# Landmark sums of five batches taken from a second load of q and k

## The chip, the cores and the metric

The kernel runs on one NeuronCore of a Trainium2 chip. Its engines are TensorE (PE in the profile; its weight loads, PEld, overlap its products), VectorE (DVE), ScalarE (ACT), GpSimd (POOL) and SyncE (SP), and 16 DMA engines that move data between HBM and SBUF. The metric is the device time of one execution in microseconds (us); lower is better. The kernel before took 270.38 us, the median of three runs of 268.30, 270.38 and 270.43 us.

## The reference

Nyström attention over 8 batches of 8 heads, 576 tokens and 64 features, then a two-layer feed-forward with a squared ReLU over 4,608 tokens, all in float32 at the interface. Cut to what matters:

```python
m = 32                                                   # landmarks: 576 / 32 = 18 tokens each
q_lm = q.reshape(B, H, m, S // m, D).mean(axis=3)
k_lm = k.reshape(B, H, m, S // m, D).mean(axis=3)
A  = softmax(scale * q @ k_lm.T)                         # 576 x 32
Bm = softmax(scale * q_lm @ k_lm.T)                      # 32 x 32
C  = softmax(scale * q_lm @ k.T)                         # 32 x 576
Z = Bm.T / (norm1(Bm) * norminf(Bm) + 1e-6)              # norms over the last two axes
for _ in range(6): Z = 2 * Z - Z @ Bm @ Z
attn = A @ Z @ C @ v                                     # heads side by side: 512 features
h = attn @ w_in; r = maximum(h, 0); out = (r * r) @ w_out   # 512 -> 2048 -> 512
```

The change is about the first step, the mean over each 18 neighbouring tokens: it makes the 32 landmarks of every head.

## The kernel before

The work goes batch by batch. The 8 heads of a batch sit as four heads by two halves `r`: 128 partitions are four heads (`c`) of 32 segments each, and one partition holds the 18 tokens of its segment side by side, 18 x 64 elements. `load_qk` brings q or k of one half into the tile `X` in that form (`ldq5.1` is q of batch 5, half 1), cast to bf16 on the way. `X` has three buffers, so batches 3 and 6 use that of batch 0. `load_v` does the same for v (`ldv5.10`), `load_win` and `load_wout` load the weights. All loads are issued by POOL, in the order of its program, and run through one software DMA queue; the finished rows of the output go out through SP's queue.

For a batch `b` the steps are:

- `lm{b}`: landmark sums on PE. The 18 tokens of a partition are added by products with an identity, in the 64x64 tiling of the array: 36 products of 256 columns (line 480, `X` against `ident`), which leave two half sums in different partitions. `lmc` (two copies, line 379 on ACT or 383 on DVE, into `LS`) and `lme` (line 498 on DVE) add them and scale; `lmt` transposes them into `LT`. Batches 0 and 1 do some of this in the full array (line 473).
- `T{b}`: four 32x32-block transposes of `X` into `TT` on DVE (line 441).
- `B{b}` and the small steps behind it: softmax and norm of the 32 x 32 matrices; then six rounds of the iteration, `N{b}.i` on PE (line 666) and `U{b}.i` on DVE (line 680). From batch 2 on each round needs `bd{b}.i`, a block-diagonal copy that POOL or DVE makes (line 603).
- `SS{b}`: the scores for A and C on PE (lines 697, 702), their softmaxes on DVE and ACT; `CV{b}` (line 788) is C v, `ZC{b}` Z times that, and `W{b}` in four chunks (line 859) its product with `w_in`, copied to `WP`: the first layer then multiplies A by `WP` and the attention output is never formed.
- `F{b}`: the first layer on PE (line 1023), `R` the ReLU (line 1037 on ACT, 1039 on DVE), `Q` its square (1044, 1046); `O{t}`: the second layer for output tile `t` of 128 tokens, four groups of four products (line 1063), `Oe` the copy out of PSUM, `St` the store.

What runs in which order is written out by hand: the string `ORDER` names every step, PE's products of one batch between the chains of the next. `Plan.schedule` walks through it with a table of costs, gives each step a start on its engine, and the instructions are emitted by these starts; so each engine executes one fixed sequence, and an engine whose next instruction has to wait holds up all behind it. A load can only be issued by POOL when its buffer is free and when the load eight places before it has landed (`SW_LANES`). Until the first `O` the plan puts dummy products (`fill`, line 1137) into PE's gaps.

`add_landmarks` and `landmarks_added`, another way to make the sums, stand in the file before, but no batch uses them (`ADDED` is empty).

Of the kernel before, what the change touches and what calls it, by code (L numbers as in the profile page):

```python
# [7 lines left out]
P = 128  # L8
# [8 lines left out]
H = 8  # L17
S = 576
D = 64
# [34 lines left out]
class Plan:  # L54
# [42 lines left out]
    def schedule(self, order):  # L97
# [5 lines left out]
        for word in order:  # L103
# [33 lines left out]
            if o.queue == "hw":  # L137
                o.end = free[e] + (self.LANDS_LOADED if t < LOADED else self.LANDS)
            elif o.nbytes:
                sw = max(sw, free[e] + 0.5)  # L140
                sw += o.nbytes / (RATE["sw"] if sw < 23.0 else RATE["later"])
                o.end = sw + LAND
                landed.append(o.end)
# [37 lines left out]
RATE = {"sw": 0.375e6, "later": 0.405e6, "hw": 0.2e6}  # L181
# [55 lines left out]
def kernel(  # L237
# [13 lines left out]
    def mk(name, shape, dt):  # L251
        return sb.tile(shape, dt, name=name, tag=name)
# [17 lines left out]
    LD = [mk(f"LD{i}", [P, 2, 2, 6, D], F32) for i in range(2)]  # L270
# [30 lines left out]
    ident = mk("ident", [P, P], BF16)  # L301
    blk2 = mk("blk2", [P, 2, M], BF16)
# [25 lines left out]
    def c_sel(e):  # L328
# [4 lines left out]
                                channel_multiplier=-1)  # L333
    op("c5", {"POOL": 0.5}, c_sel, R=["onesf"], W=["msel"])
# [58 lines left out]
    def add_landmarks(b):  # L393
        for s in range(SEG // 6):
            for t in range(2):
                src = (q, k)[t][b].rearrange("(r c) (m s) d -> (c m) r (s d)", r=2, s=SEG)
                kd = ("LD", b % 2, t)

                def add(e, s=s, t=t, src=src):
                    nc.gpsimd.dma_start(LD[b % 2][:, t].rearrange("p r j d -> p r (j d)"),  # L400
                                        src[:, :, 384 * s:384 * s + 384],
                                        **({"accum_op": ALU.add} if s else {}))
                op(f"la{b}.{s}{t}", {"POOL": 0.74}, add, R=[kd] if s else [], W=[kd],
                   nbytes=900000 if s else 425000, queue="sw")
# [26 lines left out]
    def attention(b):  # L431
# [17 lines left out]
        def landmarks_added():  # L449
            ls = LS[i2].rearrange("p r n -> p (r n)")[:, 0:256].rearrange("p (t r d) -> p t r d", t=2, d=D)  # L450
            ld, kd, kS = LD[i2], [("LD", i2, t) for t in range(2)], ("LS", i2, 0)
            for t in range(2):
                op(f"lmc{b}.{t}", {"DVE": v_(384), "POOL": g_(384)}, lambda e, t=t: eng(e).tensor_tensor(
                    ld[:, t, :, 0:3], ld[:, t, :, 0:3], ld[:, t, :, 3:6], ALU.add),
                   R=[kd[t]], W=[kd[t]], port=("POOL", "DVE"))
                op(f"lmd{b}.{t}", {"DVE": v_(128), "POOL": g_(128)}, lambda e, t=t: eng(e).tensor_tensor(
                    ls[:, t], ld[:, t, :, 0], ld[:, t, :, 1], ALU.add),
                   R=[kd[t]], W=[(kS, t)], port=("POOL", "DVE"))
                op(f"lmf{b}.{t}", {"DVE": v_(128), "POOL": g_(128)}, lambda e, t=t: eng(e).tensor_tensor(
                    ls[:, t], ls[:, t], ld[:, t, :, 2], ALU.add),  # L460
                   R=[kd[t], (kS, t)], W=[(kS, t)], port=("POOL", "DVE"))
            op(f"lme{b}.0", {"ACT": 0.36, "DVE": 0.25}, lambda e: copy(e, lm[:], ls, scale=LMS),
               R=[(kS, 0), (kS, 1)], W=[("LM", i2, r) for r in range(2)])
# [636 lines left out]
    def loads(what, b):  # L1100
# [9 lines left out]
        elif what == "la":  # L1110
            add_landmarks(b)
# [9 lines left out]
    for b in range(B):  # L1121
        if b in ADDED:
            loads("la", b)
# [29 lines left out]
ADDED = ()  # L1153
# [16 lines left out]
c0 ldq0.0 c1 c17 Bce0@4 c12 ldk0.0 ldq0.1 ldk0.1 c5 c6 ldk1.0 ldq1.1 ldk1.1 c2 ldq1.0 c15 c9 c13  # L1170
T0.00 c3 lm0.0@5 T0.10 lme0.0/D lmt0.0 SC0.0@6 T0.01 T0.11 lm0.1@0 lmc0.10 Cmx0.0 Cex0.0 c11 win01
ldv0.11 ldv0.10 lmc0.11/D lme0.1 lmt0.1 bk0/P ldv0.00 win30 win10 win11 win00 ldv1.00 win31 ldq2.1
win21 ldq2.0 T1.10 B0@2 Bmx0 Bsb0 T1.01 Bex0 SC0.1@0 Cmx0.1 Cex0.1 Bsu0 Brc0 SA0.0@7 Amx0.0b Bml0
Bmb0 Asb0.0b Aex0.0b Btr0 SA0.1@2 Amx0.1b Bcs0 CT0.0 Asu0.0b Bnm0 Crc0 Amx0.1a Brn0 c10 Cmk0
BBT0@0 Arc0.0b Yi0 Zi0 T1.00 lm1.0@6 N0.0@0 U0.0 N0.1@0 lme1.0 lmt1.0 Amx0.0a bk1/P win20 ldk2.1
ldk2.0 ldv1.10 ldv1.11 U0.1 B1@4 Aml0.0b Bmx1 N0.2@6 U0.2 Asb0.0a Bsb1 Asb0.1a CT0.1 Aex0.0a CR0@1
CRe0/A Bex1 Aex0.1a c14/A N0.3@4 U0.3 Asu0.0a Bsu1 N0.4@5 U0.4 N0.5@0 Brc1 Arc0.0a Bml1 Asb0.1b
Aex0.1b Bmb1 U0.5 Blo1 Btr1 CV0@4,6 CVe0.1/A Aml0.0a Zd0@1 Zm0 Asu0.1a Bcs1@0 BBT1@3 Ap0.0@7 Bnm1
Arc0.1a Bad1 Aml0.1a Asu0.1b Brn1 Arc0.1b Zi1 Yi1 T1.11 CVe0.0/A ZC0@5 Ab0.0/A SA1.1@0 ZCe0 W0.0@6
We0.01 We0.00 N1.0@3 U1.0 Aml0.1b Amx1.1 W0.1@4 We0.1 N1.1@3 U1.1 Ap0.1@6 Ab0.1/A SA1.0@2 Asb1.1  # L1180
Aex1.1 N1.2@3 U1.2 Amx1.0 SC1.0@6,4 Cmx1.1 wout0 wout1 F0.2@0 R0.2 N1.3@3 U1.3 Cex1.1 F0.0@0 R0.0
# [120 lines left out]
```

## Time and profile before

| | us |
|---|---|
| median of three runs | 270.38 (268.30 to 270.43) |
| the profiled execution: its time | 271.93 |
| its span, first to last instruction | 270.2 |
| PE busy in it | 250.8 |
| DVE, ACT, POOL busy | 211.9, 186.5, 61.3 |
| granted PE clock, mean | 0.994 |

The span is 1.7 us shorter than the execution's time, and that execution took 1.55 us more than the median. "Busy" counts the time in which at least one instruction runs. The profile's views used below are: the page with its groups by line; the waits, by what ended each idle stretch of an engine; the chain of work that ended last, in order of time; the timeline of one engine; tables of windows (busy time of each engine in a stretch, then the granted PE clock, the DMA share and the GB/s written); and the DMA's packets and bytes in a window.

### The profile page before, as it was taken

How to read it: one execution, taken by the hardware profiler on the slowest of the kernel's cores; microseconds unless marked ns; L12 is line 12 of the kernel's file. 1: busy time of each engine (PE TensorE's matmuls, PEld its weight loads, DVE VectorE, ACT ScalarE, POOL GpSimd, SP SyncE). 2: the span in 40 equal slices, each digit the busy share in tenths (PEclk: the TensorE clock that was granted, in tenths of full speed). 3: DMA queues.
4: the chain of work that ended last, by engine and by line, in shares of the span. 5: the costliest groups of instructions: out<-in, count | busy, mean ns of one | idle time of the engine just before them, and what ended most of it. 6: DMA issues, size and time to landing. Idle time of an engine off the chain costs nothing.

```text
span 270.2 us, 7623 instructions
## 1 busy us (share of the span) xinstructions
PE 250.8 (93%) x3111; PEld 143.2 (53%) x3149; DVE 211.9 (78%) x562; ACT 186.5 (69%) x334; POOL 61.3 (23%) x101
## 2 busy tenths in 40 slices
PE   6888899999999499999999999999999999999993
PEld 2455566475454256546455656556454565556542
DVE  3799997867999659968998999897999988662320
ACT  1344797799594579778597688889773887795121
POOL 8366495623250000130201101002201000000000
PEclk9999999999999989999999999999999999999999
DMA  6999999979599470359410433003244300006145
GB/s 108 203 187 207 208 207 208 206 135 181 114 168 217 107 126 2 52 86 226 100 41 2 76 90 71 13 0 83 61 100 67 96 2 2 0 0 154 43 98 136
DMA packets 17282, 28.27 MB, mean 105 GB/s; under 512 B 2272, under 2 KB 6624, under 8 KB 17248
## 3 DMA queue, kind: packets, MB, share of 16 engines
q0 software_dynamic: 11328, 18.35, 41.1%
q1 hardware_dynamic: 5840, 9.38, 13.1%
q8 instruction: 24, 0.39, 0.6%
q10 hardware_dynamic: 80, 0.07, 0.1%
q14 instruction: 10, 0.08, 0.1%
HBM read 36.70 MB, written 9.44 MB: 171 GB/s over the span
## 4 chain that ended last, share of the span: by engine, by line
PE 62%; DVE 14%; DMA 10%; ACT 5%; issue 4%; POOL 3%; POOLq 0%; ACTq 0%; DVEq 0%
PE ps L1063 34%; PE ps L1023 18%; DMA X<-in_q_dram 10%; ACT RS L1037 3%; PE ps L859 3%; POOL X L390 2%; PE ps L788 1%; DVE ST L680 1%; PE ps L480 1%; DVE SA L976 1%; DVE sm L740 1%; DVE RS L1039 1%; PE ps L702 1%; DVE smA L979 1%; PE ps L666 1%
## 5 line engine op out<-in xcount | busy, mean ns | idle before, releaser
L1063 PE MATMUL ps<-w_out,G 128*128 128x512 bf16 (+1 forms) x558 | 134.1, 374 | 3.6 <-issue 2.1
L1063 PEld LDWEIGHTS <-G 128*128 128x128 bf16 x592 | 54.8, 98 | 56.4 <-issue 7.9
L1023 PE MATMUL ps<-AT,WP 128*128 128x288 bf16 (+2 forms) x512 | 75.5, 288 | 0.7 <-ACT RS L1037 0.5
L1037 ACT ACTIVATE RS<-ps 128x576 bf16<-128x576 f32 (+2 forms) x95 | 59.7, 652 | 15.1 <-PE ps L1023 13.9
L1023 PEld LDWEIGHTS <-WP 128*128 128x128 bf16 x512 | 48.4, 98 | 22.5 <-issue 2.8
L1044 ACT ACTIVATE G<-RS 128x576 bf16<-128x576 bf16 (+2 forms) x74 | 49.5, 683 | 7.8 <-DVE RS L1039 7.0
L377 ACT CAST WP<-ps 128x1024 bf16<-128x1024 f32 (+1 forms) x30 | 28.0, 972 | 5.1 <-PE ps L859 3.5
L1039 DVE TENSOR_SCALAR RS<-ps 128x576 bf16<-128x576 f32 (+1 forms) x33 | 24.3, 744 | 7.1 <-PE ps L1023 5.6
L1046 DVE TENSOR_TENSOR G<-RS 128x576 bf16<-128x576 bf16 (+2 forms) x45 | 19.9, 452 | 12.3 <-ACT RS L1037 11.9
L441 DVE STREAM_TRANSPOSE TT<-X 128x576 uint32<-128x576 uint32 x32 | 24.2, 762 | 3.6 <-DMA X<-in_q_dram 2.6
L603 POOL TENSOR_TENSOR BD<-ST,blkb 128x256 bf16<-128x256 bf16 x13 | 9.1, 704 | 78.3 <-DVE ST L680 72.7
L377 ACT COPY OS<-ps 128x512 f32<-128x512 f32 (+2 forms) x26 | 14.6, 561 | 15.6 <-PE ps L1063 14.9
L743 ACT ACTIVATE C<-ps,sm 128x576 bf16<-128x576 f32 x16 | 14.4, 905 | 8.3 <-DVE sm L740 8.0
L680 DVE SCALAR_TENSOR_TENSOR ST<-ST,ps 128x128 bf16<-128x128 bf16 (+1 forms) x48 | 12.7, 265 | 8.0 <-PE ps L666 6.6
L412 POOL DMA_DIRECT2D V<-in_v_dram x24 | 12.9, 539 | 15.5 <-PE ps L788 12.0
L381 DVE COPY OS<-ps 128x512 f32<-128x512 f32 (+1 forms) x12 | 7.8, 647 | 10.3 <-PE ps L1063 6.6
L390 POOL DMA_DIRECT2D X<-in_k_dram x16 | 9.0, 561 | 17.3 <-DVE sm L754 16.1
L740 DVE TENSOR_REDUCE sm<-ps 128x1 f32<-128x576 f32 x16 | 11.8, 742 | 0.8 <-PE ps L702 0.8
L1137 PE MATMUL ps<-onesb 128*128 128x512 bf16 (+1 forms) x35 | 10.3, 406 | 2.0 <-DVE onesb L319 1.5
L379 ACT ACTIVATE LS<-ps 64x256 f32<-64x256 f32 (+1 forms) x8 | 2.9, 366 | 12.1 <-PE ps L480 12.0
L480 PE MATMUL ps<-X,ident 64*64 64x256 bf16 (+1 forms) x252 | 7.8, 264 | 3.6 <-DMA X<-in_q_dram 3.1
L390 POOL DMA_DIRECT2D X<-in_q_dram x16 | 9.2, 573 | 8.2 <-DVE sm L597 5.5
(131 smaller groups left out, 298.9 us busy)
## 6 DMA issues: line engine op xcount, KB each, us to landing
out_dram<-OS SPq DMA_DIRECT2D x70, 128.0 KB, 2.6
X<-in_q_dram POOLq DMA_DIRECT2D x16, 288.0 KB, 7.2
X<-in_k_dram POOLq DMA_DIRECT2D x16, 288.0 KB, 7.6
V<-in_v_dram POOLq DMA_DIRECT2D x8, 288.0 KB, 6.6
w_in<-in_moe_w_in_dram POOLq DMA_DIRECT2D x8, 256.0 KB, 10.0
w_out<-in_moe_w_out_dram POOLq DMA_DIRECT2D x4, 512.0 KB, 10.8
V<-in_v_dram POOLq DMA_DIRECT2D x8, 216.0 KB, 5.3
V<-in_v_dram POOLq DMA_DIRECT2D x8, 72.0 KB, 2.6
```

Source lines behind the costliest of these rows:

```text
L377: nc.scalar.copy(o, i)
L390: lambda e: nc.gpsimd.dma_start(x[:, t, r].rearrange("p s d -> p (s d)"), src),
L441: op(f"T{b}.{t}{r}", {"DVE": v_(576)}, lambda e, r=r: nc.vector.transpose(tt[:, t, r].rearrange("p s m e -> p (s m e)").bitcast(U32), x[:, ...
L680: nc.vector.scalar_tensor_tensor(out=o, in0=i0, scalar=2.0, in1=bank(pN)[:, 0:2 * w].rearrange("p (r w) -> p r w", r=2), op0=ALU.mult, op1 ...
L740: op(f"Cmx{b}.{r}", {"DVE": v_(576)}, lambda e, r=r: nc.vector.tensor_reduce(s_[:, 12 + r:13 + r], cbanks(r), axis=AX.XY, op=ALU.max, nega ...
L743: op(f"Cex{b}.{r}", {"ACT": a_(576) + 0.27}, lambda e, r=r: nc.scalar.activation(Cs[r][:].rearrange("p x u -> p u x"), cbanks(r), AF.Exp, ...
L1023: nc.tensor.matmul(ps[:, ph.at + i, 0:w], lhsT=wp[:, r, 128 * ff:128 * ff + 128], rhs=at[:, r, t0:t0 + w], start=(r == 0), stop=(r == 1))
L1037: nc.scalar.activation(rs, pair(ph, w), AF.Relu)
L1039: nc.vector.tensor_scalar(out=rs, in0=pair(ph, w), scalar1=0.0, scalar2=None, op0=ALU.max)
L1044: nc.scalar.activation(g, rs, AF.Square)
L1046: eng(e).tensor_tensor(g, rs, rs, ALU.mult)
L1063: nc.tensor.matmul(bank(po)[:, 0:c1 - c0], lhsT=G[:, f, lo:lo + P], rhs=w_out[:, f, c0:c1], start=(f == 0), stop=(f == NF - 1))
```

## The change

For batches 3 to 7 (`ROWS`) the landmark sums no longer come from `X`. A new load, `lx{b}.0` for q and `lx{b}.1` for k, brings the whole of q and of k a second time, in another form, into a new tile `XS` of 96 partitions: partition `p` holds tokens 6p to 6p + 5 of each of the 8 heads. Three neighbouring partitions are then one segment. `lm{b}.0` becomes 24 products in the 128x32 tiling (four column tiles, one for each head `c`): the stationary operand is `seg`, a 96 x 32 matrix of ones and zeros, the moving one token of the six for that head of q and k and both halves, 256 columns, and six products add up in one PSUM bank. One copy with a scale, `lme`, takes the result to `LM`; the two `lmc` copies and the addition are gone for these batches. `XS` has one buffer: `lx4` can only be issued when `lm3` is done. `X` is still loaded for all batches, for the transposes. `LD`, a tile of the unused way, is removed and has the same size in total.

Beside it the plan's table gets a third, lower rate for loads after 48 us, and `ORDER` is searched anew: all 1,420 words of it stand elsewhere, in the early part too. In it the half r = 1 of batch 0 comes first, and of the block-diagonal copies 25 are on POOL where 15 were (on DVE 17 where 27 were). ACT gets 97 of the ReLU steps where it had 95 and 78 of the squares where it had 74.

```diff
-RATE = {"sw": 0.375e6, "later": 0.405e6, "hw": 0.2e6}
+RATE = {"sw": 0.375e6, "hw": 0.2e6, "first": 0.375e6, "then": 0.405e6, "late": 0.29e6}
...
-    LD = [mk(f"LD{i}", [P, 2, 2, 6, D], F32) for i in range(2)]
+    XS = mk("XS", [96, 2, H, 6, D], BF16)
...
+    def load_xs(b):
+        for t in range(2):
+            src = (q, k)[t][b].rearrange("h (p j) d -> p h (j d)", j=6)
+            op(f"lx{b}.{t}", {"POOL": 0.57}, lambda e, t=t, src=src: nc.gpsimd.dma_start(
+                XS[:, t].rearrange("p h j d -> p h (j d)"), src),
+               W=[("XS", t)], nbytes=1179648, queue="sw")
...
+        def landmarks_rows():
+            pl_ = Bank(1, "att")
+            view = lambda: bank(pl_)[:, 0:256].rearrange("p (t r d) -> p t r d", t=2, d=D)
+
+            def lmx(e):
+                xs = XS[:].rearrange("p t (r c) j d -> p t r c j d", r=2)
+                for j in range(6):
+                    for c in range(4):
+                        nc.tensor.matmul(view()[quad(c)], lhsT=seg[:], rhs=xs[:, :, :, c, j, :],
+                                         start=(j == 0), stop=(j == 5))
+            op(f"lm{b}.0", {"PE": pe(256, 6) + 0.11}, lmx, R=["seg", ("XS", 0), ("XS", 1)], W=[pl_],
+               alloc=[pl_], mode="128x32", ni=48)
+            op(f"lme{b}.0", {"ACT": 0.1 + ap_(256), "DVE": v_(256)},
+               lambda e: copy(e, lm[:], view(), scale=LMS), R=[pl_], W=[("LM", i2, r) for r in range(2)])
...
-            if b in ADDED:
-                landmarks_added()
+            if b in ROWS:
+                landmarks_rows()
...
     for b in range(B):
-        if b in ADDED:
-            loads("la", b)
+        if b in ROWS:
+            loads("xs", b)
...
-ADDED = ()
+ROWS = (3, 4, 5, 6, 7)
...
-c0 ldq0.0 c1 c17 Bce0@4 c12 ldk0.0 ldq0.1 ldk0.1 c5 c6 ldk1.0 ldq1.1 ldk1.1 c2 ldq1.0 c15 c9 c13
+c0 ldq0.1 c1 c2 ldk0.1 c3 lm0.1@2 lmc0.10 c12 T0.01 c17 Bce0@5 ldq0.0 ldk0.0 ldq1.0 ldk1.0 c5
```

PE's sequence where the sums of batch 4 begin. Before, they follow the second chunk of `W2` and read `X_63`, the buffer of batch 4:

```order
2399 L859 Ldweights ZC_0_92
2400 L859 Matmult ps<-w_in,ZC_0_92 32x512
2401 L859 Ldweights ZC_1_93
2402 L859 Matmult ps<-w_in,ZC_1_93 32x512
2403 L480 Ldweights ident
2404 L480 Matmult ps<-X_63,ident 64x256
2405 L480 Ldweights ident
2406 L480 Matmult ps<-X_63,ident 64x256
```

With the change they follow the first round of batch 3's iteration (`N3.0`), ahead of `W2`, and read `XS`:

```order
2337 L666 Ldweights BD_101
2338 L666 Matmult ps<-ST_0_99,BD_101 128x64
2339 L666 Ldweights BD_101
2340 L666 Matmult ps<-ST_0_99,BD_101 128x64
2341 L458 Ldweights seg
2342 L458 Matmult ps<-XS,seg 32x256
2343 L458 Ldweights seg
2344 L458 Matmult ps<-XS,seg 32x256
```

So the product that the next batch hangs on now stands ahead of `W2` instead of behind half of it, and needs another load.

POOL's sequence of loads before that point. Before, behind the block-diagonal copy for batch 3 (row 60); `X_63` is batch 4's buffer, `X_62` batch 6's, `X_64` batch 5's:

```order
60 L603 TensorTensor BD_103<-Bt_114,blkb 128x256
61 L412 DMACopy V_67<-in_v_dram 96x1152
62 L412 DMACopy V_66<-in_v_dram 128x1152
63 L390 DMACopy X_64<-in_k_dram 128x1152
64 L412 DMACopy V_65<-in_v_dram 96x1152
65 L390 DMACopy X_62<-in_q_dram 128x1152
66 L390 DMACopy X_62<-in_k_dram 128x1152
67 L390 DMACopy X_63<-in_q_dram 128x1152
68 L390 DMACopy X_64<-in_k_dram 128x1152
69 L390 DMACopy X_63<-in_q_dram 128x1152
70 L390 DMACopy X_63<-in_k_dram 128x1152
```

With the change (row 64 is the same copy; rows 61 and 63 are `lx4.0` and `lx4.1`, rows 69 and 71 `lx5.0` and `lx5.1`):

```order
60 L413 DMACopy V_67<-in_v_dram 96x1152
61 L403 DMACopy XS<-in_q_dram 96x8x384
62 L413 DMACopy V_65<-in_v_dram 128x1152
63 L403 DMACopy XS<-in_k_dram 96x8x384
64 L603 TensorTensor BD_102<-Bt_113,blkb 128x256
65 L397 DMACopy X_63<-in_k_dram 128x1152
66 L397 DMACopy X_63<-in_q_dram 128x1152
67 L603 TensorTensor BD_101<-ST_0_99,blkb 128x256
68 L397 DMACopy X_64<-in_q_dram 128x1152
69 L403 DMACopy XS<-in_q_dram 96x8x384
70 L603 TensorTensor BD_102<-ST_1_100,blkb 128x256
71 L403 DMACopy XS<-in_k_dram 96x8x384
72 L413 DMACopy V_66<-in_v_dram 96x1152
```

Where nine loads stood in one piece behind the copy, the two for batch 4's sums now stand ahead of it, two of batch 4's four `X` loads behind it, and the rest are spread between copies.

More of the change, by code (lines that the diff above doesn't have):

```diff
@@ L140, in schedule @@
                 sw = max(sw, free[e] + 0.5)
-                sw += o.nbytes / (RATE["sw"] if sw < 23.0 else RATE["later"])
+                sw += o.nbytes / RATE["first" if sw < 23.0 else "then" if sw < 48.0 else "late"]
                 o.end = sw + LAND
@@ L1175 @@
[L1175 to L1180, printed above, removed]
```

223 lines of the change are left out of this document (105 added, 118 removed).

## The prediction

> **What bounds the kernel now.** I read the page first, then PE's waits after its first second-layer product, then the chain around the one long wait.
>
> ```profile
> PE 250.8 (93%) x3111; PEld 143.2 (53%) x3149; DVE 211.9 (78%) x562; ACT 186.5 (69%) x334; POOL 61.3 (23%) x101
> PEclk9999999999999989999999999999999999999999
> ...
> PE ps L480 <- DMA X<-in_q_dram: 3.1, 1, 3.1
> PE ps L1063 <- issue: 2.1, 12, 0.3
> ...
> 44.42 0.59 PE ps L1063 x2
> ...
> 77.31 14.98 DMA X<-in_q_dram
> 92.54 1.18 PE ps L480 x36
> ...
> 113.94 1.11 PE ps L480 x36
> 115.04 0.56 PE ps L859 x16
> ...
> 135.37 0.49 PE ps L1023 x4
> 135.86 1.73 PE ps L1063 x8
> ```
>
> PE is busy 93% of the span. From 44.42 us, the first `O`, it waits 3.1 us once for a load and 2.1 us in twelve scraps of at most 0.3 us: from there on the kernel lasts as long as PE's work plus that one hole. The hole is `lm4.0` at 92.54 us: it needs all of batch 4's `X`, and the last part, q of half 0, took 15 us from its issue. The table of 1-us windows shows the hole and what follows; columns are the length, PE, PEld, DVE, ACT and POOL busy, the granted PE clock, the DMA share and GB/s.
>
> ```profile
> 89.00:90.00 1.00, 0.39 (x16) 0.09 (x7) 1.00 (x3) 0.98 (x2) 0.00 (x0) 1.00 0.97 250
> 90.00:91.00 1.00, 0.00 (x0) 0.00 (x0) 0.55 (x2) 1.00 (x2) 0.00 (x0) 1.00 0.42 103
> 91.00:92.00 1.00, 0.00 (x0) 0.00 (x0) 0.00 (x0) 0.16 (x1) 0.00 (x0) 1.00 0.12 25
> 92.00:93.00 1.00, 0.46 (x17) 0.49 (x21) 0.68 (x1) 0.00 (x0) 0.00 (x0) 1.00 0.00 0
> 93.00:94.00 1.00, 0.71 (x28) 0.57 (x21) 0.96 (x4) 0.24 (x1) 0.00 (x0) 0.84 0.07 16
> 94.00:95.00 1.00, 0.96 (x3) 0.40 (x3) 0.14 (x1) 0.14 (x1) 0.98 (x2) 0.50 0.09 23
> 95.00:96.00 1.00, 1.00 (x5) 0.50 (x4) 0.00 (x0) 0.43 (x1) 0.09 (x1) 0.50 1.00 150
> 96.00:97.00 1.00, 1.00 (x6) 0.60 (x4) 0.00 (x0) 0.57 (x2) 0.00 (x0) 0.50 0.97 99
> 97.00:98.00 1.00, 1.00 (x10) 0.75 (x9) 0.53 (x2) 0.75 (x3) 0.00 (x0) 0.95 1.02 171
> ```
>
> PE stands still from 89.39 to 92.54 (3.15 us). Then its clock falls to half: 0.84, 0.50, 0.50, 0.50 and 0.95 in five windows are 1.71 us of missing clock, of which I count 1.6, since PE was idle for part of the first. The hole costs **4.75 us** in all.
>
> [...]
>
> **Part 1: the products.** Five times 36 products (1.11 to 1.18 us in the chain, mean 1.15) give way to five times 24. Four column tiles should run side by side, as eight small tiles do in line 859: 16 products of 512 columns in 0.56 us, where one after the other four products of 288 columns take 0.49 us, so 16 of 512 would take 3.5. Six rounds of 256 columns are then 6 x 0.109 (0.49 / 4 x 256 / 288) = 0.65 us; the old form had 9 x 0.109 = 0.98 and took 0.17 more, so I take 0.82. Bounds: 0.65, and 24 x 0.109 = 2.6 if they don't overlap at all. Gain 5 x 0.33 = **1.65 us**, all on PE's path; at 2.6 it would be a loss of 7.3.
>
> **Part 2: the hole.** `lm4.0` no longer waits for `X`. It needs `lx4.0` and `lx4.1`, which stand ahead of the long row of loads. Whether the hole closes or only moves is a question of the queue:
>
> ```profile
> DMA packets 815, 1.66 MB, mean 184 GB/s; under 512 B 89, under 2 KB 89, under 8 KB 815
> q0 software_dynamic: 763, 1.56, 101.9%
> ...
> DMA packets 1648, 1.66 MB, mean 208 GB/s; under 512 B 51, under 2 KB 1644, under 8 KB 1646
> ...
> q0 software_dynamic: 11328, 18.35, 41.1%
> q1 hardware_dynamic: 5840, 9.38, 13.1%
> ...
> V<-in_v_dram POOLq DMA_DIRECT2D x8, 72.0 KB, 2.6
> ```
>
> The first two rows are 76 to 85 us, where only `X` and `v` were loaded: 1.56 MB in 9 us, 173 GB/s, so an `X` part of 0.295 MB takes 1.7 us. The third is 39 to 47 us, packets of 1 KB (`w_out`): 208 GB/s. An `lx` is 768 packets of 768 bytes, 0.59 MB: 2.9 us at 205 GB/s, **3.4 us** at 173, which I take. The far bound is the mean over all software packets: 41.1% of 16 x 270.2 us by 11,328 is 157 ns each, 7.5 us for 768 of them on 16 engines. Output rows take 13.1% of 270.2 us, 35 us spread over the 225 behind 44 us: 16%, so I divide by 0.84. A small load lands 2.6 us after issue, 0.4 of it bytes: 2.2 us fixed.
>
> When each sum is due comes from adding the PE rows above, and those of the other groups, along the new order from its first `O` (which stands behind 26.1 us of PE work, before behind 25.9, so I leave it at 44.4): `lm3.0` at 62.6, `lm4.0` 87.9, `lm5.0` 103.1, `lm6.0` 149.0, `lm7.0` 169.6. (The same addition over the old order gives 90.5 for `lm4.0`, where the trace, without the hole, has 89.4.)
>
> - `lx3.1`: about 34.5 `X` parts' worth is queued up to it, against 30.2 up to `wout3`, whose bytes end near 47; two `lx` and a quarter part behind it land by 57. Margin 6 us.
> - `lx4.1`: from 62.5 us there are 4.75 parts of `X` and v and two `lx`: (4.75 x 1.7 + 2 x 3.4) / 0.84 + 2.2 puts it at 82. Margin 5 us.
> - `lx5.1` is the tight one. `lx5.0` can't be issued before `lm4.0` has read `XS`. Between the two stand 15.2 us of PE work (6 groups of `O`, 11 `F`, 4 chunks of `W`, 5 rounds `N`, `B4`, `CV3`, `lm4`); the queue needs 0.6 + 2.2 + (1.7 + 2 x 3.4) / 0.84 = 12.9. Margin 2.3 us: it holds up to 4.4 us for an `lx`.
> - `lx6.0` and `lx7.1` hold up to 4.9 and 5.2 us by the same sum.
>
> [...]
>
> So both items of the hole go: **4.75 us**. What comes next late? PE's other waits came to 2.5 us over 225, and I take 0.7 us for waits of the new order that the old one lacked (bounds 0, and 4.75 for another hole of that size).
>
> **Part 3: what lies beside.** Costed at nothing:
>
> ```profile
> L379 ACT ACTIVATE LS<-ps 64x256 f32<-64x256 f32 (+1 forms) x8 | 2.9, 366 | 12.1 <-PE ps L480 12.0
> L390 POOL DMA_DIRECT2D X<-in_q_dram x16 | 9.2, 573 | 8.2 <-DVE sm L597 5.5
> L427 POOL DMA_DIRECT2D w_out<-in_moe_w_out_dram x4 | 3.1, 771 | 1.9 <-DMA X<-in_q_dram 1.2 <-DMA w_in<-in_moe_w_in_dram 0.6
> L603 POOL TENSOR_TENSOR BD<-ST,blkb 128x256 bf16<-128x256 bf16 x13 | 9.1, 704 | 78.3 <-DVE ST L680 72.7 <-DVE Btf L549 5.6
> L603 DVE TENSOR_TENSOR BD<-ST,blkb 128x256 bf16<-128x256 bf16 x23 | 6.5, 281 | 0.4
> ...
> 130.00:140.00 10.00, 9.89 (x114) 4.94 (x104) 9.54 (x25) 7.05 (x14) 1.05 (x3) 1.00 0.42 95
> 190.00:200.00 10.00, 9.79 (x116) 4.99 (x116) 9.90 (x24) 7.64 (x14) 1.84 (x3) 1.00 0.48 102
> ```
>
> Ten `lmc` copies of 0.37 us go and the chain from `lm` to `B` gets shorter; ACT and DVE have this room already. Ten block-diagonal copies move from DVE (0.28 us) to POOL (0.70): DVE loses 2.8 us of work, ten rounds get 0.42 us longer each, hidden by the `O` and `F` groups between `N`s; without that cover 4.2 us. DVE is the engine near its limit (9.54 and 9.90 of 10 us), and it only gets lighter. Ten more loads cost POOL some 0.9 us each (0.57 at 128 rows, 0.77 at 512, on that slope 0.91 at 768): 9 us on an engine that is busy 23%. But POOL is in order: a load that waits for `lm`, or for the load eight places back, now stands ahead of more block-diagonal copies. DMA share falls to 0.42 and 0.48 in the two windows, so 34 us more of loads fit.
>
> In the first 44 us the same loads run ahead of `wout3`, the halves of batch 0 change places, and one block copy of 1.2 us goes from POOL to DVE. I take 0, bounds 1.4 either way (one `X` part in the queue).
>
> **Sum**, against the profiled execution: 271.93 - 1.65 - 4.75 + 0.7 = 266.2 us. That execution took 1.55 us more than the median, so the forecast is **264.7 us**. Its own range, from the bounds of products, head and waits without a new hole, is 262 to 267.
>
> **Rivals.**
>
> - *The hole moves.* A sum or a transpose waits 3 us or more somewhere else, most likely at `lm5.0` (margin 2.3 us) or where DVE takes `T4.01`, whose load comes some eight parts later. It gives back 2 to 4.75 us and some of the next engine's time: 267 to 270. For it: the old order, too, was laid out for its loads to be in time and missed by 3 us. Against: the new order has a lower rate for late loads, and the margins above.
> - *Slow short packets (slower).* At L us for an `lx`, `lm5`, `lm6` and `lm7` each wait 2.38 us for every us above 4.4, 4.9 and 5.2. At 5.6 us the gain of 5.7 is gone; at 6.0 it is 273; at the far bound of 7.5 these three alone cost 7.4 + 6.2 + 5.5 = 19 us, 284. Only the mean per packet speaks for it; the 1-KB window speaks against, 78 ns a packet (8 us x 16 / 1,646), which is 3.7 us.
> - *The change doesn't do what it says*: the four column tiles run one after the other. Then 7.3 us lost where I have 1.65 gained: 273.7. Line 859's rows speak against it, though they show 64-row tiles.
> - *More gain*: no new waits and an earlier head, 261 to 262.
>
> **How the numbers follow.** The forecast 0.62, the moved hole 0.18, slow packets 0.10, serial tiles 0.05, more gain 0.05. A measurement here tells some 1% from no change: under 267.7 is faster, over 273.1 slower. Faster: forecast, more gain and a small part of the moved hole, 0.70. Within 1%: the rest of it and the mild end of slow packets, 0.17. Slower: the rest, 0.13. Forecast and moved hole hold 0.80: 261.5 to 270.
>
> **What would show it.** Right: no PE wait over 1 us after the first `O`; clock 1.00 around 90 us; the new products in 0.7 to 0.9 us; `XS` landing 6 to 8 us after issue when queued. Wrong: a wait of PE for `XS` or of DVE for `X`, with a half-clock stretch behind it; products near 2.6 us; the first `O` later than 46 us; POOL's copies late behind a waiting load.

## The result and the profile after

The changed kernel takes 267.97 us, the median of 20 runs (265.46 to 269.84); the kernel before, run beside it, took 270.40 (20 runs, 268.30 to 274.24). The ratio is 0.9913, with a 95% interval of 0.9888 to 0.9938: 2.4 us faster. (The ratios here and below leave out single runs that lie more than 1.5% above the fastest of the same kernel.) The prediction was 264.7 us, 5.7 us faster than before, in a range of 261.5 to 270.0. The direction and that range hold; the narrower range of 262 to 267, for a change without a new hole, doesn't. Less than half of the gain came: 267.97 lies within 1% of the time before, to which the prediction gave 0.17.

The profiled execution of the change took 268.07 us, its span is 266.3. First the page's rows for the engines and for the granted PE clock, then PE's waits from 40 us to the end (us in total, times, longest):

```profile
PE 254.8 (96%) x3090; PEld 140.4 (53%) x3090; DVE 210.7 (79%) x539; ACT 185.9 (70%) x339; POOL 75.1 (28%) x121
...
PEclk9799999999999999999999999999999999999999
```

```profile
PE ps L1023 <- DVE AT L996: 0.3, 1, 0.3
PE ps L1023 <- ACT CV L384: 0.2, 1, 0.2
```

Behind the first `O` PE waits 0.5 us in all: the hole at `lm4.0` is gone and no other took its place. The dip of the clock that stood at 92 us is gone too. There is a new one, in the second slice of the span, ahead of 14 us. The chain that ended last (start, length, what) shows what came before it, and the new products:

```profile
2.36 6.80 DMA X<-in_k_dram
9.30 0.70 PE ps L480 x36
...
63.48 0.77 PE ps L458 x24
...
89.77 0.77 PE ps L458 x24
```

The sums take 0.77 us where the old form took 1.11 to 1.18. The chain's first piece is the second load of the program, k of batch 0: issued at 2.36, landed at 9.16. The timeline of the kernel before has the start of the transpose that reads that load, and PE's first `O`; the timeline of the change has the same two rows (start, length, engine, line, operation, and in brackets the idle time ahead and what ended it):

```profile
7.10 0.78 DVE L441 STREAM_TRANSPOSE TT<-X 128x576 uint32<-128x576 uint32 x1 [0.47 <-DMA X<-in_k_dram]
...
43.99 1.02 PE L1063 MATMUL ps<-w_out,G 128*128 128x512 bf16 x3 [0.22 <-ACT RS L1037]
```

```profile
9.19 0.78 DVE L442 STREAM_TRANSPOSE TT<-X 128x576 uint32<-128x576 uint32 x1 [2.75 <-DMA X<-in_k_dram]
9.30 0.70 PE L480 MATMUL ps<-X,ident 64*64 64x128 bf16 x36 [2.19 <-DMA X<-in_k_dram]
...
45.94 1.03 PE L1063 MATMUL ps<-w_out,G 128*128 128x512 bf16 x4
```

The load comes 2.1 us later, PE stands still for 2.2 us for it, and the first `O` comes 1.95 us later. (The 44.42 of the prediction was a piece of the chain that starts inside the first group; by the timeline that group starts at 43.99, and from here on all kernels are read by the timeline.) The windows of the change, in the prediction's columns, show the clock at half speed for 3.4 us, from 1 us behind the end of the stall:

```profile
10.00:11.00 1.00, 1.00 (x5) 0.46 (x6) 0.68 (x4) 0.27 (x1) 0.23 (x2) 0.63 1.07 196
11.00:12.00 1.00, 1.00 (x7) 0.16 (x8) 0.90 (x2) 0.00 (x0) 0.80 (x3) 0.50 1.14 214
12.00:13.00 1.00, 1.00 (x17) 0.40 (x16) 0.00 (x0) 0.00 (x0) 0.54 (x1) 0.50 1.10 207
13.00:14.00 1.00, 1.00 (x13) 0.67 (x10) 0.82 (x2) 0.03 (x1) 0.34 (x1) 0.67 1.08 205
```

So the time splits at the first `O`. Before it lies the **head**: 43.99 us before, 45.94 now. Behind it lies the **stretch** to the end of the span: 270.2 - 43.99 = 226.2 before, 266.3 - 45.94 = 220.4 now. The stretch gained 5.8 us and the head gave 1.95 back.

### The profile page after: what moved, and what is told of

It is laid out like the page before. It is cut to its first block, busy times and chain, and to the rows that moved or that the text cites. A ratio compares the mean times of both kernels' runs of the same rounds, so it can differ in the third digit from the quotient of the medians.

```text
span 266.3 us, 7555 instructions
## 1 busy us (share of the span) xinstructions
PE 254.8 (96%) x3090; PEld 140.4 (53%) x3090; DVE 210.7 (79%) x539; ACT 185.9 (70%) x339; POOL 75.1 (28%) x121
## 4 chain that ended last, share of the span: by engine, by line
PE 73%; DVE 13%; ACT 6%; issue 3%; DMA 3%; POOL 0%; DVEq 0%; POOLq 0%; ACTq 0%
PE ps L1063 40%; PE ps L1023 20%; ACT RS L1037 3%; DMA X<-in_k_dram 3%; PE ps L859 2%; PE ps L702 2%; DVE TT L442 2%; PE ps L788 2%; ACT G L1044 2%; PE ps L1137 1%; DVE sm L740 1%; DVE WP L388 1%; DVE ST L680 1%; PE ps L666 1%; DVE An L938 1%
## 5 line engine op out<-in xcount | busy, mean ns | idle before, releaser
L1063 PE MATMUL ps<-w_out,G 128*128 128x512 bf16 (+1 forms) x592 | 138.5, 374 | 0.1
L1023 PEld LDWEIGHTS <-WP 128*128 128x128 bf16 x512 | 47.9, 98 | 23.8 <-issue 4.3
L1044 ACT ACTIVATE G<-RS 128x576 bf16<-128x576 bf16 (+2 forms) x78 | 52.3, 687 | 0.7
L603 POOL TENSOR_TENSOR BD<-ST,blkb 128x256 bf16<-128x256 bf16 x21 | 14.9, 710 | 85.6 <-DVE ST L680 44.1
L1039 DVE TENSOR_SCALAR RS<-ps 128x576 bf16<-128x576 f32 (+2 forms) x31 | 23.1, 754 | 5.4 <-PE ps L1023 5.1
L384 ACT CAST WP<-ps 128x1024 bf16<-128x1024 f32 (+1 forms) x25 | 22.8, 949 | 3.3 <-PE ps L859 3.2
L1137 PE MATMUL ps<-onesb 128*128 128x512 bf16 (+1 forms) x40 | 14.1, 470 | 1.8 <-DVE onesb L320 1.5
L976 DVE STREAM_TRANSPOSE SA<-ps 128x320 f32<-128x320 f32 (+1 forms) x24 | 10.1, 459 | 3.5 <-PE ps L697 2.4
L603 POOL TENSOR_TENSOR BD<-Bt,blkb 128x256 bf16<-128x256 bf16 x4 | 3.0, 744 | 30.9 <-DVE sm L597 15.0
L1046 POOL TENSOR_TENSOR G<-RS 128x512 bf16<-128x512 bf16 (+1 forms) x8 | 8.8, 1101 | 9.3 <-DVE RS L1039 5.9
L388 DVE CAST WP<-ps 128x1024 bf16<-128x1024 f32 x9 | 10.8, 1205 | 0.8 <-PE ps L859 0.8
```

The source lines that it names most:

```text
L384: nc.scalar.copy(o, i)
L388: eng(e).tensor_copy(o, i)
L603: bdiag = lambda e, o, i: eng(e).tensor_tensor(o.rearrange("p r (c m) -> p r c m", c=4), i.unsqueeze(2).to_broadcast([P, 2, 4, M]), blkb[: ...
L1023: nc.tensor.matmul(ps[:, ph.at + i, 0:w], lhsT=wp[:, r, 128 * ff:128 * ff + 128], rhs=at[:, r, t0:t0 + w], start=(r == 0), stop=(r == 1))
L1039: nc.vector.tensor_scalar(out=rs, in0=pair(ph, w), scalar1=0.0, scalar2=None, op0=ALU.max)
L1044: nc.scalar.activation(g, rs, AF.Square)
```

## The experiments

Each kernel is a small edit of the kernel before or of the changed one. The table has, from the profiled execution, the issue of the program's second load, the start of the transpose that reads it, the first `O` and the stretch, and then the median of the runs.

| kernel | 2nd issue | 2nd load read | first `O` | stretch | median |
|---|---|---|---|---|---|
| before | 2.02 | 7.10 | 43.99 | 226.2 | 270.1 to 270.4 |
| `e2_q4_first` | 2.02 | 7.16 | 43.62 | 222.3 | 268.64 |
| `e3_select_early` | 2.36 | 9.12 | 47.92 | 223.1 | 273.93 |
| `e6_rows_old_order` | 2.03 | 7.10 | 45.25 | 223.4 | 270.16 |
| `e11_old_order_one_load` | 2.02 | 7.15 | 44.85 | 222.7 | 269.16 |
| the change | 2.36 | 9.19 | 45.94 | 220.4 | 267.97 |
| `a12_after_again` | 2.36 | 9.13 | 47.10 | 220.3 | 268.82 |
| `e1_select_late` | 2.03 | 6.99 | 44.05 | 220.3 | 265.73 |
| `e8_select_third` | 2.02 | 7.03 | 43.81 | 220.3 | 266.14 |
| `e9_select_first` | 2.65 | 7.55 | 44.21 | 220.5 | 266.35 |
| `e7_memset_there` | 2.17 | 8.69 | 46.47 | 220.3 | 267.03 |
| `e10_gap_only` | 2.26 | 9.27 | 46.12 | 220.7 | 268.57 |
| `e4_one_second_load` | 2.37 | 9.03 | 45.74 | 220.2 | 267.57 |
| `e5_products_twice` | 2.36 | 8.58 | 45.14 | 223.7 | 271.60 |

Third and fourth column: where the second load is read by 7.6 us the first `O` comes at 43.6 to 45.3, where it is read at 8.6 or later, at 45.1 to 47.9. Part of the spread within each group goes with the granted clock. Of the seven profiles with the load on time, four lose none of it ahead of the first `O` (`e2_q4_first`, `e8_select_third` and `e9_select_first` with a mean of 1.000 over the span, the kernel before with 1.00 in every window up to 46 us) and have the first `O` at 43.6 to 44.2. The other three have it at 44.05 (`e1_select_late`, at half clock from 27.2 to 30.6 us), 44.85 (`e11_old_order_one_load`, a mean of 0.994, with 1.00 in every window from 44 us on) and 45.25 (`e6_rows_old_order`, at half clock from 26.6 to 33.4). Of the late ones, the four latest (`e10_gap_only`, `e7_memset_there`, `a12_after_again`, `e3_select_early`) have a mean of 0.987, the others 0.993 to 0.996. What brings the half clock behind 26 us no run tries. In the windows of `e1_select_late` it looks like this:

```profile
26.00:28.00 2.00, 2.00 (x25) 1.07 (x24) 1.97 (x8) 0.58 (x1) 1.22 (x2) 0.80 1.18 206
28.00:30.00 2.00, 2.00 (x35) 0.72 (x28) 1.53 (x4) 1.82 (x3) 0.73 (x2) 0.50 1.16 205
30.00:32.00 2.00, 2.00 (x49) 1.19 (x48) 1.97 (x4) 1.29 (x3) 0.77 (x2) 0.85 1.14 209
```

Fifth column: with the new order and the new products the stretch is 220.2 to 220.7, whatever the head does.

### What made the head late

The two orders differ at the start in one thing that the prediction did not name: the select on GpSimd that makes the identity (`c2`) stands behind the seventh load before, and between the first and the second with the change. Two kernels move only that. The first moves three loads of the changed kernel ahead of it:

```diff
-c0 ldq0.1 c1 c2 ldk0.1 c3 lm0.1@2 lmc0.10 c12 T0.01 c17 Bce0@5 ldq0.0 ldk0.0 ldq1.0 ldk1.0 c5
+c0 ldq0.1 c1 ldk0.1 ldq0.0 ldk0.0 c2 c3 lm0.1@2 lmc0.10 c12 T0.01 c17 Bce0@5 ldq1.0 ldk1.0 c5 ldq1.1
```

> The changed kernel with one thing moved: the select on GpSimd that makes the identity stands behind the fourth load instead of between the first and the second; no other engine's sequence differs. Theory S (the select between the loads holds up the early queue): the second load, 6.8 us from issue to landing in the changed kernel's trace, lands near 7.1 us instead of 9.2, PE no longer waits 2.2 us for it nor falls to half clock from 10.4 to 13.6, the first O starts near 44.4 instead of 45.9, and the time falls by 1.5 us, to 266.4. Rival N (the new early order itself is longer): the load lands earlier but the first O stays near 45.9 and the time within 0.4 us of 268.0.

It took 265.73 us (6 runs, 265.29 to 266.18), 0.9833 of the time before (0.9793 to 0.9873, an interval that doesn't meet that of the change), 2.2 us less than the change, where 1.5 was expected: better than both kernels. Its timeline:

```profile
6.99 0.78 DVE L442 STREAM_TRANSPOSE TT<-X 128x576 uint32<-128x576 uint32 x1 [0.15 <-DMA X<-in_k_dram]
...
44.05 1.03 PE L1063 MATMUL ps<-w_out,G 128*128 128x512 bf16 x4
```

The load is on time again and the first `O` is where it was before the change (44.05 beside 43.99). The second does the opposite to the kernel before:

```diff
-c0 ldq0.0 c1 c17 Bce0@4 c12 ldk0.0 ldq0.1 ldk0.1 c5 c6 ldk1.0 ldq1.1 ldk1.1 c2 ldq1.0 c15 c9 c13
+c0 ldq0.0 c1 c2 c17 Bce0@4 c12 ldk0.0 ldq0.1 ldk0.1 c5 c6 ldk1.0 ldq1.1 ldk1.1 ldq1.0 c15 c9 c13
```

> The kernel before with the same select moved the other way, between the first and the second load. Theory S: the second load lands near 9.1 us instead of 7.1 and all early loads 2 us later, PE's first products start near 9.2 instead of 7.2, the first O near 46, and the time rises by 1.5 to 2 us, to 272. Rival N: the second load is late by the 0.34 us that the select takes and the time stays within 0.5 us of 270.4.

It took 273.93 us (4 runs), 1.0133 of the time before (1.0080 to 1.0185). Its timeline:

```profile
9.12 0.78 DVE L441 STREAM_TRANSPOSE TT<-X 128x576 uint32<-128x576 uint32 x1 [3.00 <-DMA X<-in_k_dram]
...
47.92 1.02 PE L1063 MATMUL ps<-w_out,G 128*128 128x512 bf16 x4 [0.23 <-ACT RS L1037]
```

The old kernel gets the same late load (9.12) and loses 3.75 us, more than the 1.5 to 2 expected. So by the medians the place of `c2` costs 2.2 us in the new order and 3.75 in the old one.

Is it the select, or any instruction there, or the pause? Four more kernels, all from the change. In `e7_memset_there` the select stands late as in `e1_select_late`, and a memset stands in its old place (`c19` in the place of `c2` in the first line of the order):

```diff
+    op("c19", {"POOL": 0.3}, lambda e: nc.gpsimd.memset(identf[:], 0.0), W=["identf"])
```

> The changed kernel with the identity's select behind the fourth load (265.7 before), and in its old place, between the first and the second load, a memset of the same tile on GpSimd. Theory S1 (it is the select, the first of the program, that holds up the loads behind it): the second load lands near 7.1 us as without anything there, plus the memset's own time, and the median stays within 0.7 us of 265.7. Rival S2 (any instruction of GpSimd between the first two loads does it): the second load lands near 9.2 and the first O comes near 46; 267.5 to 268.5.

In `e8_select_third` the select stands between the second and the third load:

```diff
-c0 ldq0.1 c1 c2 ldk0.1 c3 lm0.1@2 lmc0.10 c12 T0.01 c17 Bce0@5 ldq0.0 ldk0.0 ldq1.0 ldk1.0 c5
+c0 ldq0.1 c1 ldk0.1 c2 c3 lm0.1@2 lmc0.10 c12 T0.01 c17 Bce0@5 ldq0.0 ldk0.0 ldq1.0 ldk1.0 c5 ldq1.1
```

> The changed kernel with the second load moved ahead of the identity's select: the select then stands between the second and the third load. Theory S3 (the first select stops the making of descriptors for some 2 us, and what is already in the queue hides it): the second load lands near 7.1, the third, otherwise due at 8.9, at 9 to 10, since the 1.7 us of the second load's bytes cover most of the stop; 265.7 to 266.7. Rival S4 (the select adds its 2 us to the load behind it wherever it stands): the third lands near 10.9, and what reads it (the other half of batch 0) is 2 us late; if that half is on the path, 267.5 or more.

In `e9_select_first` it stands ahead of all loads:

```diff
-c0 ldq0.1 c1 c2 ldk0.1 c3 lm0.1@2 lmc0.10 c12 T0.01 c17 Bce0@5 ldq0.0 ldk0.0 ldq1.0 ldk1.0 c5
+c0 c1 c2 ldq0.1 ldk0.1 c3 lm0.1@2 lmc0.10 c12 T0.01 c17 Bce0@5 ldq0.0 ldk0.0 ldq1.0 ldk1.0 c5 ldq1.1
```

> The changed kernel with the identity's select ahead of all loads, none between the first two. Every load is issued some 0.6 us later (the select waits for the ones that DVE writes until 1.6 us). Theory V (what delays the second load is something standing between it and the first, not a select that was run): the second load lands 0.6 us behind 7.1, near 7.7; first O near 44.5, 266.4 or less. Rival W (the program's first select stops the loads behind it for 2 us, wherever it stands): the first load itself lands 2 us late, near 7.5, the second near 9.2; 267.9 or more.

And in `e10_gap_only` nothing stands between them on GpSimd (the select is late, as in `e1_select_late`); the second load waits for VectorE, which writes into its target first (`c19` behind `c1`):

```diff
+    op("c19", {"DVE": 0.5}, lambda e: nc.vector.memset(X[0][:, 1, 1, 0:10], 0.0), W=[("X", 0, 1, 1)])
```

> The changed kernel with the identity's select behind the fourth load (265.7) and no instruction of GpSimd between the first two loads; instead the second load waits for a memset on VectorE of part of its target, and is issued near 2.3 us instead of 2.02, as late as behind the select (2.36). Theory X (the pause between the issues does it, not the instruction): the second load lands near 9 us, as behind the select, and the median is near 267.9. Rival Y (an instruction of GpSimd is needed): it lands near 7.4, and the median is 265.7 to 266.3.

`e7_memset_there` took 267.03 us (10 runs, 265.01 to 268.48), `e8_select_third` 266.14 (4 runs, 265.37 to 267.04), `e9_select_first` 266.35 (4 runs, 266.19 to 266.42), `e10_gap_only` 268.57 (10 runs, 265.40 to 269.10). The timelines of GpSimd and VectorE, first of `e10_gap_only`:

```profile
1.31 0.72 POOL L397 DMA_DIRECT2D X<-in_q_dram  x1 [0.80 <-POOLq L1285]
2.26 0.54 POOL L397 DMA_DIRECT2D X<-in_k_dram  x1 [0.22 <-issue]
...
9.27 0.78 DVE L444 STREAM_TRANSPOSE TT<-X 128x576 uint32<-128x576 uint32 x1 [2.78 <-DMA X<-in_k_dram]
```

and then of `e9_select_first`:

```profile
1.68 0.29 POOL L322 TENSOR_SCALAR_AFFINE_SELECT identf<-onesf 128x128 f32<-128x128 f32 x1 [1.17 <-DVE onesf L321]
1.92 0.73 POOL L397 DMA_DIRECT2D X<-in_q_dram  x1
2.65 0.55 POOL L397 DMA_DIRECT2D X<-in_k_dram  x1
...
7.55 0.78 DVE L442 STREAM_TRANSPOSE TT<-X 128x576 uint32<-128x576 uint32 x1
```

The pause does it, not the select. With 0.22 us of nothing between the two issues the load lands as late as with the select there (theory X); with the select ahead of both, and the issues back to back, it is 0.56 us later than in `e1_select_late`, for an issue 0.62 us later (theory V). The memset, a pause of 0.14 us, gives the late load in its profile (8.69), and a spread of 3.5 us between its runs, so some of them seem to have escaped; a median of 267.03 lies between what its two theories said. With the pause behind the second load (`e8_select_third`) nothing is lost: the third transpose starts at 9.16, in `e1_select_late` at 9.13 (the time of theory S3, and less delay than it allowed; whether anything stops while the select runs, as the theory has it, no run shows). With two loads ahead of it the pause costs nothing, with one it does.

What the DMA does meanwhile, in half-microsecond windows of the change and then of the kernel before (the last two columns are DMA share and GB/s):

```profile
4.50:5.00 0.50, 0.50 (x3) 0.23 (x2) 0.00 (x0) 0.00 (x0) 0.50 (x2) 1.00 0.80 115
5.00:5.50 0.50, 0.50 (x3) 0.22 (x2) 0.22 (x1) 0.00 (x0) 0.43 (x4) 1.00 0.71 120
5.50:6.00 0.50, 0.50 (x3) 0.15 (x1) 0.50 (x1) 0.00 (x0) 0.50 (x2) 1.00 0.87 152
```

```profile
4.50:5.00 0.50, 0.50 (x3) 0.16 (x2) 0.40 (x3) 0.00 (x0) 0.50 (x2) 1.00 1.06 198
5.00:5.50 0.50, 0.50 (x3) 0.20 (x2) 0.00 (x0) 0.00 (x0) 0.50 (x2) 1.00 1.04 198
5.50:6.00 0.50, 0.50 (x3) 0.10 (x1) 0.26 (x1) 0.00 (x0) 0.50 (x3) 1.00 1.06 198
```

In the change the DMA engines are busy for 0.71 to 0.87 of these windows instead of all of them, and what they move falls further, from 198 GB/s to between 115 and 152. That is not what all late loads have in common: `e10_gap_only` has a share of 0.96 to 1.08 and 166 to 180 GB/s in the same windows, and its load is late all the same. The landings say more. In the traces of the kernel before and of the change each of the first loads raises its semaphore in sixteen steps. For the second load of the kernel before all sixteen come between 6.14 and 7.08 us; in the change eleven come by 7.06, one at 7.39 and the last four between 8.47 and 9.16. So there the load isn't slow as a whole: the last four of its sixteen parts come up to 2.1 us late, and its reader starts behind the last one, at 9.19. Why a pause of a third of a microsecond should hold up some of the parts no run shows, and it stays open.

The change once more, as a control for `e9_select_first` and `e10_gap_only`:

> The changed kernel once more, beside the others of this call: 267.4 to 268.5, stretch behind the first O 220.4, second load landing near 9.2 in the profile. If the late second load were only an accident of the one profile, it lands near 7.1 here and the first O comes near 44.

268.82 us (10 runs, 267.86 to 270.61), a little above what was expected, with the load late again (9.13) and the first `O` at 47.10. That is 0.9963 of the time before (0.9929 to 0.9998), so beside these runs the gain of the change is 1.0 us and not 2.4. `e9_select_first`, run beside it, has 0.9865 (0.9808 to 0.9921): the pause costs 2.5 us between these two medians, and the intervals don't meet. Not every run seems to pay: the fastest of the change took 265.46 us and the fastest of `e10_gap_only` 265.40, but no trace shows when the load came in them.

### What the hole was worth

In the kernel before, batch 4's q moved to the front of the row of loads that `lm4.0` waits for, so that the hole closes and nothing else changes:

```diff
-ldv4.00 CV2@4,0 CVe2.0/A ldk5.0 ldv3.10 ldq6.1 ldk6.0 ldq4.1 ldk5.1 ldq4.0 O6.1
+ldq4.1 ldq4.0 ldv4.00 CV2@4,0 CVe2.0/A ldk5.0 ldv3.10 ldq6.1 ldk6.0 ldk5.1 O6.1
```

> The kernel before with one thing moved: the two q loads of batch 4 stand ahead of the other seven loads of their row instead of sixth and last; no other engine's sequence differs. q of half 0 should land near 83 us instead of 92.3 and PE's wait of 3.15 us at lm4.0, with the half clock behind it, should be gone. Theory A (the hole costs each run what it cost in the profiled one, 4.75 us): 265.6, which is 2.4 us faster than the changed kernel. Rival B (the profiled execution was a bad one, in the median run the hole costs 3.15 us or less, the clock not falling each time): 267.2 to 268.5. Rival C (another load of the row is late in its turn): a new wait of PE or DVE between 90 and 130 us, and 269 to 270.

It took 268.64 us (12 runs), 0.9933 of the time before (0.9896 to 0.9970): 1.5 us between the medians, 0.8 to 2.8 by the interval. Theory A falls, and the gain is a little under what rival B allowed. PE's waits for the sums of `X` behind the first `O`, first in `e2_q4_first` and then in `e3_select_early`, which left the row of loads as it was:

```profile
PE ps L480 <- issue: 0.6, 1, 0.6
```

```profile
PE ps L480 <- DMA X<-in_q_dram: 1.6, 1, 1.6
```

The hole was 3.1 us, with half a clock behind it, in the one profile that the prediction read; in another run of the same row of loads it is 1.6 us and the clock holds (`e3_select_early`, 1.00 from 47.92 to 140 us). The stretches say the same: 226.2, 223.1, and 222.3 without the hole. So its price varies from run to run, and the profiled run seems to have drawn a high one.

### The products and the loads

The products of the change done twice, the second set starting the sum anew:

```diff
-                for j in range(6):
+                for j in [*range(6), *range(6)]:
```

> The changed kernel with the 24 products of each sum done twice, one set after the other (the second set starts the sum in PSUM anew, so the output is the same). Theory P (behind the first O the kernel lasts as long as PE's work): five times 0.77 us more, 3.85 us, so 271.8 beside the 267.97 of the changed kernel. Rival Q (PE has slack between the sums and the products lie beside it, so their time doesn't pass on): under 1 us more, at most 269. If the products' 0.77 us is mostly a fixed cost of the switch of tiling and not of the columns, each sum grows by less than 0.65 us and the total by less than 3.3.

271.60 us (10 runs), 3.6 above the change. In its chain each sum of 48 products takes 1.42 or 1.43 us:

```profile
62.68 1.43 PE ps L458 x48
89.64 1.42 PE ps L458 x48
```

The second set costs 0.65 us, five of them 3.25; the stretch grew by 223.7 - 220.4 = 3.3. PE's time passes to the end one to one. Of the 0.77 us, 0.65 go with the columns; the other 0.12 come once for each sum, and that they are the switch of tiling is not shown.

With the second loads of batch 3 only, so that the sums of batches 4 to 7 are made of batch 3's tokens and eight of the ten loads are left out:

```diff
-        if b in ROWS:
+        if b == ROWS[0]:
             loads("xs", b)
```

> The changed kernel with the second load of q and k for batch 3 alone; the sums of batches 4 to 7 are taken from batch 3's tokens, so eight of the ten loads are left out and the landmarks of those batches are other numbers. PE, DVE and ACT run the same sequences. Theory F (the loads are free, hidden behind PE): within 0.4 us of 268.0. Rival L (they cost, through the queue, POOL's order or the ports): 1 to 2 us faster, 266 to 267, with the difference to be found in PE's small gaps between 60 and 170 us.

267.57 us (8 runs), 0.9894 of the time before (0.9852 to 0.9935), and the stretch is 220.2 beside 220.4. In the new order the eight loads cost nothing that can be seen.

Then the product form and the ten loads in the old order, with its head (but for `c18`, which makes `seg`), its block copies and its ReLU steps:

```diff
-wout3 ldk3.1 ldq3.0
+wout3 lx3.0 lx3.1 ldk3.1 ldq3.0
...
-lm3.0@6 N2.2@1 lmc3.00 lmc3.01 Q1.12 U2.2
+lm3.0@6 lx4.0 lx4.1 N2.2@1 Q1.12 U2.2
...
-lm4.0@2 lmc4.00 bd3.1/D
+lm4.0@2 lx5.0 lx5.1 bd3.1/D
```

> The product form and the second loads alone, in the order of before: its words stay where they are (head, block copies, ReLU and squares too), the sums read XS, the loads for batch 3 go behind the last of w_out, those for the batches 4 to 7 right behind the sum of the batch ahead. Theory T (what the change brings behind the first O is the form of the sums and the hole, and the order searched anew brings nothing): 270.2 less 5 x 0.38 for the products and less 1.6 for the hole, 266.7, with no wait of PE over 1 us behind the first O, and a first O near 44. Rival U (the new order is needed to make room for the loads): PE waits 3 us or more for XS, or DVE for X or V; 269 or more, with a stretch of half clock behind it.

270.16 us (10 runs, 269.76 to 270.63), 1.0003 of the time before (0.9971 to 1.0034): nothing gained, and theory T falls. There is no single wait of 3 us either, as rival U had it, but several small ones that the new order doesn't have. PE's waits behind the first `O`:

```profile
PE ps L1023 <- DVE OS L388: 1.4, 1, 1.4
PE ps L1023 <- DVE RS L1039: 0.5, 1, 0.5
PE ps L666 <- ACT RS L1037: 0.4, 1, 0.4
PE ps L788 <- ACT RS L1037: 0.4, 1, 0.4
PE ps L859 <- DVE RS L1039: 0.3, 1, 0.3
```

They sum to 3.0 us, and the stretch is 223.4 where the new order has 220.4. The longest comes from a load, as its timeline shows on VectorE and then on PE:

```profile
94.48 0.78 DVE L442 STREAM_TRANSPOSE TT<-X 128x576 uint32<-128x576 uint32 x1 [1.92 <-DMA X<-in_q_dram]
95.19 0.65 DVE L388 COPY OS<-ps 128x512 f32<-128x512 f32 x1
...
95.89 0.53 PE L1023 MATMUL ps<-AT,WP 128*128 128x288 bf16 x3 [1.43 <-DVE OS L388]
```

VectorE stands 1.9 us for an `X` part, the copy out of PSUM queued behind its transpose is late, and PE waits for the bank. The same kernel without the eight loads of batches 4 to 7 (the edit of `e4_one_second_load`, and their words out of the order):

> The kernel with the product form in the order of before (270.16), with the second loads of batch 3 only: the sums of batches 4 to 7 read batch 3's tokens, and the eight loads of the other batches are left out. Theory T1 (it is the eight loads, put into the queue of the old order without making room, that cost its 3 us of waits behind the first O): these waits go, the stretch behind the first O falls from 223.4 to 220.4, and the median to 267.2. Rival T2 (the waits come from the steps of the old order around the shorter sums, not from the loads): the stretch stays at 223 or more and the median at 269.8 or more.

269.16 us (10 runs, 268.61 to 270.54), stretch 222.7. The 1.4 us are gone; the wait for a ReLU step of VectorE is now 1.1 us, and the other three are as they were:

```profile
56.38 1.44 DVE L442 STREAM_TRANSPOSE TT<-X 128x576 uint32<-128x576 uint32 x2 [1.51 <-DMA X<-in_k_dram]
...
59.41 0.60 PE L1023 MATMUL ps<-AT,WP 128*128 128x256 bf16 x4 [1.09 <-DVE RS L1039]
```

This one seems to come from the pair for batch 3, which the kernel keeps: it stands ahead of batch 3's `X` in the queue, and the two transposes wait 1.5 us for an `X` part. They start 2.6 us later than in the kernel before, 0.9 of it because the first `O` is later too:

```profile
53.77 1.43 DVE L441 STREAM_TRANSPOSE TT<-X 128x576 uint32<-128x576 uint32 x2
```

So the eight loads are worth 0.7 us by the stretch and 1.0 by the medians, whose intervals overlap, and not 3: the result lies between T1 and T2, nearer T2. Another 1.1 seems to go to the pair for batch 3, which no run leaves out. The last 1.1, three short waits for ReLU steps that both kernels show, is not traced to a load, and what makes them wasn't tried.

## Why the prediction was wrong in size

The stretch was right. The prediction's sum put the end at 266.2 - 1.73 (time less span) = 264.5 in the span and left the first `O` where it was, 43.99 by the timeline: a stretch of 220.5. It is 220.4. By its steps:

- **Part 1, the products.** Right. Taken at 0.82 us, measured 0.77; a gain of 5 x (1.15 - 0.77) = 1.9 us instead of 1.65. The two stretches without a hole, 222.3 of `e2_q4_first` and 220.4, differ by as much, though the first has 0.5 us more of waits too. The four column tiles do run side by side: the 24 products take 0.77 us, where one after the other, at the 0.109 us each of the prediction's estimate, they would take 2.6.
- **Part 2, the hole.** It closes and doesn't move; PE's waits are 0.5 us where 0.7 was taken for new ones. Its 4.75 us was nearly right for that execution (226.2 - 222.3 = 3.9, and `e2_q4_first` still has a wait of 0.6 at that place, 4.5 together) and wrong for the median, where it is 1.5. The twelve scraps of 2.1 us listed beside it were hardly waits: that profile has 558 products of line 1063 where the change's has 592, and the scraps are missing from every profile with all 592.
- **Sum, "That execution took 1.55 us more than the median, so the forecast is 264.7 us".** This is the first step that failed. The profiled execution was 1.55 us above the median, and the sum took off both the hole of that execution, at its full price, and the 1.55. That needs the change, too, to run 1.55 above its median when profiled; it ran 0.1 above (268.07 beside 267.97). The likely reason is that the excess sat in the hole, so that closing the hole took it away and the 1.55 was counted twice. The stretches argue for it: 226.2 with the long hole, 223.1 with the short one of `e3_select_early`. It isn't measured, since runs without a trace don't show where they lose time, and the half clock alone isn't it: the mean clock of that execution, 0.994, is no lower than the median of the mean clocks in the later runs of the kernel before (0.991 to 0.994).
- **Part 3, the head, "I take 0, bounds 1.4 either way".** This is the second, and the larger in what it teaches. The median of the change less 1.8 (time less span) and less the stretch of 220.4 leaves 45.8 for the first `O`: 1.8 us later than 43.99, beyond the bound. The bound was made of bytes in the queue, one `X` part; the early queue gets no more bytes, but a select of 0.3 us moves in between the first two issues. `e1_select_late` puts the price at 2.2 us. The working followed what PE waits for behind 44 us, and for the head asked only which loads come first.
- **Part 3, what lies beside.** Costed at nothing, and nothing it was: `e4_one_second_load` for the loads; for the copies on GpSimd, no wait of PE for them stands in the list above. `XS` landed later than the 6 to 8 us that were expected (KB each, median us to landing, from the page after), and no PE wait names it: the order had more room than the margins say. The prediction didn't weigh that this room was the order's work: the same products and loads in the old order gained nothing.

```profile
XS<-in_q_dram POOLq DMA_DIRECT2D x5, 576.0 KB, 11.0
XS<-in_k_dram POOLq DMA_DIRECT2D x5, 576.0 KB, 10.2
```

1.8 of the head and 1.55 taken off in vain, less 0.1 of the stretch, are the 3.25 us between 264.7 and 267.97. The 45.8 for the head is what the medians leave over, not a time that a trace shows, so the split is an estimate. By medians alone the products (1.9) and the hole (1.5) make 3.4 us, while `e1_select_late` is 4.45 faster than the kernel before: the 1.0 between them lies within the interval of `e2_q4_first`, and no run says where it goes.

Of the rivals, the moved hole, slow short packets and serial tiles are refuted by the waits and the 0.77. The sign "first `O` later than 46 us" was the right one to watch: 45.94 in one profile, 47.10 in another.

## What to carry to other kernels

Before an excess of the profiled execution over the median is subtracted, say which term of the sum holds it; if it is the term that the change removes, it may already be in. At the start of a program, where the queue is empty, read the issues of the first two loads as closely as any wait later on: in this program they belong back to back (the select between them, a pause of 0.34 us, cost 2.2 us by the medians), and what the issuing engine can do behind the second should stand there. And an order and the loads that it was laid out for are one change: without the new order, the products and their loads gained nothing.

## What the runs showed of the hardware

A pause of 0.2 to 0.35 us between the issues of the first two loads made the second land 1.5 to 2.2 us later: its reader starts at 8.6 to 9.3 in the six profiles with such a pause, at 7.0 to 7.2 in the six with none and the first issue at the same time. GpSimd need not run anything in it, and the same pause one load later cost nothing. In the change the late ones are four of the load's sixteen parts, landed at 8.47 to 9.16 us where eleven had landed by 7.06. The late load also stops PE: in those six profiles it stood still for 1.4 to 3.2 us, and in the five with 2.2 us or more the clock fell to half, during the stall or within 1 us of its end: for 3.4 us in the change, `e3_select_early` and `e4_one_second_load`, for at least 3.3 in `a12_after_again` and at least 6 in `e10_gap_only` (0.50 in every window from 9 to 15 us). In the median the old order lost 3.75 us to it and the new one 2.2. `e1_select_late`, one of the three versions that avoid it, is the fastest of all, 265.73 us.

The stretches at half clock whose two ends are seen lasted about as long as one another, or twice as long: 3.41 us in the change (10.25 to 13.66) and at the hole of the kernel before (93.69 to 97.10), 3.4 by the windows in `e1_select_late` (27.2 to 30.6), `e3_select_early` (9.2 to 12.6) and `e4_one_second_load` (10.0 to 13.4), and 6.8 in `e6_rows_old_order` (26.6 to 33.4). The length of a stall alone doesn't decide: in `e1_select_late` the clock falls at 27.2 us behind waits of at most 1.1 us, in `e5_products_twice` it holds behind a stall of 1.4. In the 3.41 us ahead of the fall PE was busy for 1.22 us in the change and for 1.15 at the hole of the kernel before. What decides when the clock falls no run tries.
